# A 2:4-sparse matrix product on one core: the second token pair's load behind a memset, tile 4 transposed before tiles 2 and 3, one 512-column dummy matmul fewer

## The chip, the core and the metric

The kernel runs on one core of one Trainium2 chip. The metric is the device time of one execution in microseconds; lower is better. Where a number stands without a unit it is microseconds, counted from the start of the profiled span.

## What is computed

`x` is 16x512 tokens of 1024 bf16 values, `w` a 1024x1024 bf16 matrix, `b` a bias of 1024. In each column of `w`, of every four rows that follow each other the two of largest magnitude are kept; then the pruned matrix multiplies the tokens:

```python
wg = w.reshape(G, M, D)                       # G = 256 groups of M = 4 rows
mag = jnp.abs(wg)
order = jnp.argsort(mag, 1)
thr = jnp.take_along_axis(mag, order[:, M - N:M - N + 1, :], 1)   # N = 2
wp = (wg * (mag >= thr)).reshape(D, D)
return jnp.einsum("bsd,df->bsf", x, wp) + b
```

## The kernel before

The 8192 tokens are 64 tiles of 128 tokens. The product of a tile is two halves of 512 output columns, each the sum of eight matmuls over 128 of the 1024 inputs. The last 48 to 50 tiles (L359 to L375) run in one regular stream: tokens come in already transposed by DMA, TensorE multiplies, VectorE adds the bias while it empties the PSUM bank, and the result is stored.

The front handles the time in which the weights aren't pruned yet. The weights are cut into six pieces (L61): pieces 0 to 3 are rows 0 to 511 in steps of 256 columns, 4 and 5 rows 512 to 1023 in steps of 512. A piece is loaded (`load_w`, L69), its magnitudes taken (`abs_piece`, L109: token A), and pruned in place on VectorE (`prep_piece`, L124: token P; L150 makes the mask, L153 applies it). Piece 0 is pruned in two halves of the group index m (0 and 1, then 2 and 3), and the first half in two column blocks, so that the first matmuls can begin early.

The first eight token tiles are not transposed by DMA but by TensorE: `load_x` (L76) loads the first 512 inputs of one or two tiles in natural order (tiles 0 and 1, tiles 2 and 3, tile 4, tile 5, tiles 6 and 7), `transpose_half` (L177, token T) makes four 128x128 transposes with an identity matrix into a PSUM bank taken in turn by `next_bank` (L53), and `copy_half` (L184, token C) brings the bank back to SBUF on ScalarE. Tokens N and M are matmuls (`mm_part`, L191): N.0.t.m multiplies piece 0 with tile t for one group index m, M does all four. N.0.t.0 and N.0.t.1 read the first half of piece 0, N.0.t.2 and N.0.t.3 the second. Token V copies a finished half to a staging buffer on ScalarE (L235); token U unpacks the pruned piece into natural row order by DMAs on SP (L172); D and G are DMA transposes on SP (`xfill`, L259, and `xg1`, L324); I loads weights.

W and w are dummy matmuls (`warm`, L104) of ones into PSUM bank 7, with 512 and 128 columns. They read nothing that is loaded and nothing reads them.

What sets the order: `K` keeps the instructions that it wraps in program order, so every engine's queue follows the text: first the loads at L83 to L91, then the small set-up (a zeroed tile, a first copy on ScalarE with its table load, the identity, which GpSimd makes), then the tokens of the string FRONT (L285), one after the other. DMAs are issued by two queues: SP has the first half of the first weight piece (128 KB), tiles 0 and 1 (256 KB), tile 4, tile 5, the second weight piece, tiles 6 and 7, and more weights; ScalarE has the other half of the first weight piece and tiles 2 and 3 (256 KB).

Of the kernel before, what the change touches and what calls it, by code (L numbers as in the profile page):

```python
# [10 lines left out]
def kernel(  # L11
# [7 lines left out]
    nc = tc.nc  # L19
    P = 128  # L20
    bf16 = mybir.dt.bfloat16
# [4 lines left out]
    K = tc.keep_in_program_order  # L26

    B, S, D = x.shape
# [10 lines left out]
    T, F = 8, 6  # L39
    NE = 8  # L40

    const = ctx.enter_context(tc.tile_pool(name="const", bufs=1))
# [30 lines left out]

    xh = {}

    def load_x(ta, tb, eng=nc.sync):  # L76
        xt = const.tile([P, tb - ta, KH], bf16, name=f"xh_{ta}")
        src = xf[ta * P:tb * P, 0:KH].rearrange("(t p) c -> p t c", p=P)
        K(eng.dma_start(xt[:], src))
        for t in range(ta, tb):  # L80
            xh[t] = xt[:, t - ta, :]

    load_w(0, 0, 256, nc.sync, 0, 2)  # L83
    load_w(0, 0, 256, nc.scalar, 2, 4)
    load_x(0, 2)
    load_x(2, 4, nc.scalar)
    load_x(4, 5)
    load_x(5, 6)
    load_w(0, 256, 512)
# [4 lines left out]
    xg1 = const.tile([P, 4, T * P], bf16, name="xg1")  # L94

    ones = nc.const_aps.tensor(1.0, (P, FH), bf16)
    zeros = const.tile([P, 16], bf16, name="zeros")
    K(nc.vector.memset(zeros[:], 0.0))
    act_first = const.tile([P, 16], bf16, name="act_first")
    K(nc.scalar.copy(act_first[:], zeros[:]))  # L100
    ident = const.tile([P, P], bf16, name="ident")
    make_identity(nc, ident[:])

    def warm(n):  # L104
        K(nc.tensor.matmul(bank[7][:, :n], lhsT=ones[:, :P], rhs=ones[:, :n], start=True, stop=True))  # L105
# [160 lines left out]
    def issue_batch(t0, nb):  # L266
# [16 lines left out]


    FRONT = """  # L285
        I.1.0.512 D.0 A.0 P.0 W W W W W W W W W w w T.0 T.1 C.0 T.2 T.3 C.1 w T.4 C.2 N.0.0.0 N.0.0.1 T.5
        N.0.1.0 N.0.1.1 N.0.0.2 N.0.0.3 N.0.1.2 N.0.1.3 M.0.2 A.1 C.3 P.1 U.0.0.0.512 I.1.512.1024 G C.4 C.5
        M.0.3 N.0.4.0.1 T.6 T.7 C.6 N.0.4.2.3 C.7 A.2 M.0.5 M.0.6 P.2 M.0.7 N.1.0.0.1 N.1.1.0.1 A.3
        N.1.2.0.1 N.1.0.2.3 N.1.1.2.3 N.1.2.2.3 V.0.0 M.1.3 V.0.1 M.1.4 V.0.2 M.1.5 M.1.6 V.0.3 M.1.7 V.0.4
# [114 lines left out]
```

## Time and profile before

| | |
|---|---|
| median of 3 runs | 233.38 us (232.98 to 233.41) |
| profiled execution | 232.85 us, of which the span is 231.1 |
| TensorE busy | 226.7 us, 98% of the span |
| VectorE, ScalarE, GpSimd busy | 52%, 8%, under 1% |
| first dummy / first transpose / first matmul of real work | 0.77 / 4.78 / 6.38 us |
| loads of the first weight piece, issue to landing | 2.6 us (SP), 2.8 us (ScalarE) |
| loads of tiles 0 and 1 and of tiles 2 and 3, issue to landing | 3.4 us (SP), 3.8 us (ScalarE), both issued at 1.25 |
| bytes moved from 2.25 to 4.20 us | 339 GB/s |

How to read it: the profile is of one execution, which is faster than the median of the runs by 0.53. A group of matmuls in a timeline shows its start and the time until the end of the last; the starts inside a group are as far apart as the matmuls need at the current clock, and a single matmul's length (379 ns for 512 columns) holds the run through the array as well, so that neighbours overlap. The chain of what ended last counts from end to end instead. An idle engine that is not on that chain costs nothing.

### The profile page before, as it was taken

To read this page: it belongs to the slowest core of one execution; us is meant where nothing else is said; L and a number is where in the kernel's file an instruction comes from. 1 tells how busy PE (TensorE), PEld (TensorE's weight loads), DVE (VectorE), ACT (ScalarE), POOL (GpSimd) and SP (SyncE) were. 2 spreads that over 40 slices of the span, in tenths; PEclk is the share of its full clock that TensorE was granted. 3 is DMA by queue.
4 is the path that set the end of the run, shared out by engine and by line. 5 is a ranking of instruction groups with operands and counts; after the bars stand their busy time and mean duration, and the time that the engine had idled before them with its cause. 6 is when DMAs were issued, how large, how long until landed. Compare 5 with 4: busy or idle time off the path is not lost.

```text
span 231.1 us, 2772 instructions
## 1 busy us (share of the span) xinstructions
PE 226.7 (98%) x1137; PEld 111.1 (48%) x1156; DVE 120.2 (52%) x213; ACT 18.0 (8%) x33; POOL 0.7 (0%) x6
## 2 busy tenths in 40 slices
PE   8999999999999999999999999999999999999995
PEld 4887444444444444444444444444444444444443
DVE  4999787867987424424424424424423423433434
ACT  3868400000000000000000000000000000000000
POOL 1000000000000000000000000000000000000000
PEclk9999999999999999999999999999999999999999
DMA  6989989999447222991249522696128950122222
GB/s 214 299 180 262 210 195 197 289 247 318 185 182 272 91 84 80 272 249 59 80 115 278 152 95 91 129 245 194 70 91 197 241 197 34 60 91 91 91 94 91
DMA packets 77228, 38.19 MB, mean 165 GB/s; under 512 B 63136, under 2 KB 69024, under 8 KB 77216
## 3 DMA queue, kind: packets, MB, share of 16 engines
q1 hardware_dynamic: 67568, 20.88, 41.4%
q10 hardware_dynamic: 9648, 17.14, 20.1%
q8 instruction: 9, 0.15, 0.3%
q14 instruction: 3, 0.02, 0.0%
HBM read 3.41 MB, written 16.78 MB: 87 GB/s over the span
## 4 chain that ended last, share of the span: by engine, by line
PE 98%; DVE 0%; issue 0%
PE bank L369 73%; PE bank L203 16%; PE bank L263 6%; PE bank L105 2%; PE bank L182 1%; DVE o_last L354 0%
## 5 line engine op out<-in xcount | busy, mean ns | idle before, releaser
L369 PE MATMUL bank<-wp_nat,xTb 128*128 128x512 bf16 x737 | 161.7, 379 | 0.8
L248 DVE TENSOR_TENSOR o_pair<-bank,bias_sb 128x512 bf16<-128x512 f32 x104 | 67.3, 687 | 99.5 <-PE bank L369 94.1
L369 PEld LDWEIGHTS <-xTb 128*128 128x128 bf16 x752 | 73.6, 98 | 88.7
L239 DVE TENSOR_TENSOR stage<-bank,stage 128x512 f32<-128x512 f32 x22 | 14.2, 687 | 4.3 <-PE bank L203 4.2
L203 PE MATMUL bank<-w,xT 128*128 128x256 bf16 x128 | 14.5, 273 | 0.0
L243 DVE TENSOR_TENSOR o_pair<-stage,bias_sb 128x512 bf16<-128x512 f32 x22 | 14.0, 684 | 0.0
L203 PE MATMUL bank<-wp_nat,xg 128*128 128x512 bf16 x62 | 13.9, 379 | 0.1
L203 PEld LDWEIGHTS <-xT 128*128 128x128 bf16 x128 | 12.3, 98 | 1.6
L235 ACT COPY stage<-bank 128x512 f32<-128x512 f32 x22 | 11.5, 613 | 4.5 <-PE bank L203 4.5
L203 PE MATMUL bank<-wp_nat,xfill 128*128 128x512 bf16 x47 | 10.6, 379 | 0.1
L263 PE MATMUL bank<-wp_nat,xfill 128*128 128x512 bf16 x47 | 10.5, 379 | 0.1
L203 PEld LDWEIGHTS <-xg 128*128 128x128 bf16 x64 | 6.3, 98 | 7.6
L263 PEld LDWEIGHTS <-xfill 128*128 128x128 bf16 x48 | 4.7, 98 | 5.7
L203 PEld LDWEIGHTS <-xfill 128*128 128x128 bf16 x48 | 4.7, 98 | 5.5
L369 PE MATMUL bank<-wp_nat,xTs 128*128 128x512 bf16 x32 | 7.1, 379 | 0.0
L150 DVE TENSOR_TENSOR mask<-mag,thr 128x512 bf16<-128x512 bf16 (+3 forms) x10 | 5.6, 584 | 0.2
L153 DVE TENSOR_TENSOR w<-w,mask 128x512 bf16<-128x512 bf16 (+3 forms) x10 | 5.6, 582 | 0.1
L105 PE MATMUL bank<-const-bfloat16-1.0 128*128 128x512 bf16 (+1 forms) x12 | 4.4, 540 | 0.8 <-PEq L388 0.8
L369 PEld LDWEIGHTS <-xTs 128*128 128x128 bf16 x32 | 3.1, 98 | 3.8
L187 ACT COPY xT<-bank 128x512 bf16<-128x512 bf16 x8 | 4.1, 605 | 2.7 <-PE bank L182 2.7
L120 DVE TENSOR_SCALAR mag<-w 128x512 uint16<-128x512 uint16 (+2 forms) x6 | 2.7, 466 | 2.5 <-DMA w<-in_w_dram 2.5
L263 PE MATMUL bank<-wp_nat,xTb 128*128 128x64 bf16 (+3 forms) x40 | 3.7, 251 | 0.0
(20 smaller groups left out, 27.1 us busy)
## 6 DMA issues: line engine op xcount, KB each, us to landing
out_dram<-o_pair ACTq DMA_DIRECT2D x25, 512.0 KB, 2.8
out_dram<-o_pair ACTq DMA_DIRECT2D x13, 256.0 KB, 2.1
wp_nat<-w SPq DMA_DIRECT2D x16, 128.0 KB, 2.9
w<-in_w_dram SPq DMA_DIRECT2D x3, 512.0 KB, 5.5
xh<-in_x_dram SPq DMA_DIRECT2D x2, 256.0 KB, 4.1
xh<-in_x_dram ACTq DMA_DIRECT2D x1, 256.0 KB, 3.8
xh<-in_x_dram SPq DMA_DIRECT2D x2, 128.0 KB, 3.6
w<-in_w_dram SPq DMA_DIRECT2D x1, 256.0 KB, 4.0
```

What stands on the lines that cost most here:

```text
L105: K(nc.tensor.matmul(bank[7][:, :n], lhsT=ones[:, :P], rhs=ones[:, :n], start=True, stop=True))
L120: K(nc.vector.tensor_single_scalar(mag[:, ms].bitcast(u16), w_of(i)[:, ms].bitcast(u16), 0x7FFF, op=Alu.bitwise_and))
L150: K(nc.vector.tensor_tensor(mask[:, ms, c], mag[:, ms, c], tb, op=Alu.is_ge))
L153: K(nc.vector.tensor_tensor(w_of(i)[:, ms, c], w_of(i)[:, ms, c], mask[:, ms, c], op=Alu.mult))
L187: K(nc.scalar.copy(xt[:], src))
L203: K(nc.tensor.matmul(dst, lhsT=lhs, rhs=rhs, start=c0 == 0 and m == 0, stop=c1 == FH and m == 3))
L235: K(nc.scalar.copy(stage[(h, t)][:], bank[own[(h, t)]][:]))
L239: K(nc.vector.tensor_tensor(st, bank[own[(2 + h, t)]][:], st, op=Alu.add))
L243: K(nc.vector.tensor_tensor(get_o(t)[:, f], stage.pop((h, t))[:], bias_sb[:, f], op=Alu.add))
L248: K(nc.vector.tensor_tensor(get_o(t)[:, f], bank[bk][:], bias_sb[:, f], op=Alu.add))
L263: K(nc.tensor.matmul(bank[bk][:, :c1 - c0], lhsT=xN[t][:, kt, :], rhs=wp_nat[h][:, kt, c0:c1], start=kt == 0, stop=kt == KT - 1))
L369: K(nc.tensor.matmul(bank[bks[h]][:], lhsT=xN[t][:, kt, :], rhs=wp_nat[h][:, kt, :], start=kt == 0, stop=kt == KT - 1))
```

## The change

- `load_x` can put a memset of the whole tile (128 partitions x 1024 bf16) on GpSimd ahead of the load. The load of tiles 2 and 3 does so; since both write the same tile, the load, which stays in ScalarE's queue, waits for the memset.
- The identity, the zeroed tile and ScalarE's first copy move up ahead of that load in the text, and so in the queues of GpSimd, VectorE and ScalarE.
- In FRONT, nine 512-column dummies become eight; the three 128-column dummies stay. The copy of tile 0 follows its transposes at once (on another engine: the order on each engine is as before), the small third dummy comes after tile 1, and tile 4 is transposed before tiles 2 and 3, so tile 4 takes the third PSUM bank and tiles 2 and 3 the fourth and the fifth.

```diff
-    def load_x(ta, tb, eng=nc.sync):
+    def load_x(ta, tb, eng=nc.sync, behind=False):
         xt = const.tile([P, tb - ta, KH], bf16, name=f"xh_{ta}")
+        if behind:
+            K(nc.gpsimd.memset(xt[:], 0.0))
         src = xf[ta * P:tb * P, 0:KH].rearrange("(t p) c -> p t c", p=P)
         K(eng.dma_start(xt[:], src))
...
     load_x(0, 2)
-    load_x(2, 4, nc.scalar)
+    ident = const.tile([P, P], bf16, name="ident")
+    make_identity(nc, ident[:])
+    zeros = const.tile([P, 16], bf16, name="zeros")
+    K(nc.vector.memset(zeros[:], 0.0))
+    act_first = const.tile([P, 16], bf16, name="act_first")
+    K(nc.scalar.copy(act_first[:], zeros[:]))
+    load_x(2, 4, nc.scalar, behind=True)
     load_x(4, 5)
...
     ones = nc.const_aps.tensor(1.0, (P, FH), bf16)
-    zeros = const.tile([P, 16], bf16, name="zeros")
-    K(nc.vector.memset(zeros[:], 0.0))
-    act_first = const.tile([P, 16], bf16, name="act_first")
-    K(nc.scalar.copy(act_first[:], zeros[:]))
-    ident = const.tile([P, P], bf16, name="ident")
-    make_identity(nc, ident[:])
...
-        I.1.0.512 D.0 A.0 P.0 W W W W W W W W W w w T.0 T.1 C.0 T.2 T.3 C.1 w T.4 C.2 N.0.0.0 N.0.0.1 T.5
+        I.1.0.512 D.0 A.0 P.0 W W W W W W W W w w T.0 C.0 T.1 C.1 w T.4 T.2 T.3 C.2 N.0.0.0 N.0.0.1 T.5
```

## Prediction

> **What bounds the kernel now.** I read the page first (busy shares, chain that ended last), then the chain in order of time, then each engine's timeline over the first 14 us. The chain:
>
> ```profile
> PE 98%; DVE 0%; issue 0%
> ...
> 0.77 4.21 PE bank L105 x11
> 4.99 1.28 PE bank L182 x16
> ...
> 6.54 0.22 PE bank L203 x2
> 6.76 0.22 PE bank L182 x4
> 6.99 1.75 PE bank L203 x16
> ```
>
> Columns: start, length, what. TensorE is the chain from its first dummy (L105) to the end, through transposes (L182) and matmuls (L203 and later), with no piece of another engine until the last tile. So the change counts only through when TensorE can begin its real work, and by whether it stops somewhere. The start, TensorE's and VectorE's timelines:
>
> ```profile
> 0.77 4.21 PE L105 MATMUL bank<-const-bfloat16-1.0 128*128 128x512 bf16 x11 [0.77 <-PEq L388]
> 4.78 1.48 PE L182 MATMUL bank<-ident,xh 128*128 128x128 bf16 x16
> 6.10 0.22 PE L105 MATMUL bank<-const-bfloat16-1.0 128*128 128x128 bf16 x1
> 6.38 0.38 PE L203 MATMUL bank<-w,xT 128*128 128x256 bf16 x2
> 6.82 1.91 PE L203 MATMUL bank<-w,xT 128*128 128x256 bf16 x16
> ...
> 3.35 0.51 DVE L120 TENSOR_SCALAR mag<-w 128x512 uint16<-128x512 uint16 x2 [2.47 <-DMA w<-in_w_dram]
> 5.66 0.49 DVE L153 TENSOR_TENSOR w<-w,mask 128x256 bf16<-128x256 bf16 x2
> 6.52 0.43 DVE L153 TENSOR_TENSOR w<-w,mask 128x512 bf16<-128x512 bf16 x1
> ```
>
> Two chains meet. VectorE waits 2.47 us for the first weight loads and then prunes without a gap: the first half of piece 0 is ready at 5.66+0.49 = 6.15, the second at 6.52+0.43 = 6.95. TensorE needs the first half at 6.38 (N.0.0.0, 0.23 to spare) and the second at N.0.0.2, the third of the sixteen: 6.82 + 2x0.109 = 7.04 (1.75/16 = 0.109 each), so 0.09 to spare. This 0.09 is the tightest place I find: **TensorE and VectorE are both nearly the bound here**. The next pieces have more: piece 1 is pruned by 10.27 and used from 10.57 and 11.22 on.
>
> **The clock in these rows.** 9 dummies of 512 columns and 2 of 128 (38 units of 128) lie between 0.77 and 4.78: 0.106 a unit, 0.42 a large dummy. The matmuls of 256 columns after 7 us take 0.109, 0.055 a unit. So TensorE starts at half rate. The 16 transposes take 6.10-4.78 = 1.32 = 0.106n + 0.055(16-n), n = 8.6: the rate doubles at about 5.69.
>
> **The dummy.** One 512-column dummy goes (9 become 8; the three small ones stay): the transposes can start 0.42 earlier, at 4.36. Tiles 0 and 1, the small dummy and tile 4 are 13 units at 0.106, up to the step at 5.69: 5.72. Tiles 2 and 3 are 8 units at 0.055: 6.16. So N.0.0.0 could start at 6.16, 0.22 earlier (half of 0.42, since work moves from full rate to half rate). But the first half is ready at 6.15 and, 0.66 of TensorE work later, the second at 6.95: N.0.0.2 would be reached at 6.82 to 6.86 and starts between 6.95 and 7.0. **Gain 0.04 to 0.09; I take 0.06.** The rest of the 0.22 becomes a new wait for VectorE, since nothing in the change starts VectorE earlier: both weight loads are first in their queues.
>
> **The first pair.** Its weights are read from 4.72 and its load lands 3.4 us after 1.25, at 4.67: only 0.05 to spare, and it is now wanted at about 4.30. In the trace its packets share the 16 engines with the second pair's from about 3.2 on. Without those 256 KB before it ends (at the 339 GB/s of the stretch 2.25 to 4.20, up to 0.77 us; some two thirds had gone, 0.5) it lands near 4.15. Bounds: 4.67, unchanged (TensorE then stands out the 0.42 of the dummy, and the 0.06 is not gained), and 3.9, all 0.77 earlier. I take 4.15: no cost.
>
> **The second pair's load.** ScalarE and GpSimd:
>
> ```profile
> 1.25 0.52 ACTq L79 DMA_DIRECT2D xh<-in_x_dram  x1
> 1.79 1.28 ACT L100 ACT_TABLE_LOAD   x1 [1.79 <-issue]
> 3.09 0.20 ACT L100 COPY act_first<-zeros 128x16 bf16<-128x16 bf16 x1
> ...
> 0.34 0.10 POOL L388 MEMSET const-uint8-127<- 128x1 uint8 x1
> 0.73 0.21 POOL masks.py:197 MEMSET ident<- 128x128 bf16 x1 [0.29 <-POOLq L388]
> 1.01 0.29 POOL masks.py:199 TENSOR_SCALAR_AFFINE_SELECT ident<-ident 128x128 bf16<-128x128 bf16 x1
> ```
>
> It moves behind the table load and the first copy on ScalarE's queue: 1.25+1.28 = 2.53, +0.20 = 2.73, so it is issued at 2.6 to 2.75. The memset (128x1024) is not in the trace. From 0.10 for 1 element a partition and 0.21 for 128, 1024 give 0.10+1023x0.00087 = 0.98: done at 1.30+0.98 = 2.28, before ScalarE asks, so this wait would cost nothing of its own. Ends: 0.21 (length without effect), and eight times the select's 0.29, 2.3, done at 3.64. Nearest is the memset row; I take 0.98. From issue to landing the trace has 2.1 us (a store of 256 KB from the same queue, later, alone) to 4.7 (the slowest load of x). I take 2.1 plus 0.77 for as many bytes of other loads that share the engines, 2.87: it **lands at about 5.6**, wanted at 5.72. Earliest 2.6+2.1 = 4.7; latest 3.64+4.7 = 8.3. Behind it on ScalarE nothing stands until the copies of tiles 0 and 1 (at 5.0 and 5.5), whose place comes after its issue.
>
> **The rest at nothing.** The identity moves no work: GpSimd has it at 1.30, wanted at 4.3. Tile 4 before 2 and 3 gives it the third PSUM bank; that bank is emptied by the fifth of the eight copies of L235 (from 11.64, 0.48 apart: by 14.2) and taken again at 14.9. SP's first DMA transpose (5.38) carries in its record a wait on the semaphore that the second pair raises. Landing at 5.6 to 6 holds SP for 0.2 to 0.6, and with it the unpacking, the next weights and the xg transpose behind it. xfill lands at 5.38+9.9 = 15.3 for a first use at 20.9, xg at 15.88+7.2 = 23.1 for 26.0: 2.9 cover it. The memset's zeros are overwritten by the load.
>
> **Sum.** The profiled execution took 232.85 (span 231.1 and 1.75 around it): 232.85-0.06 = 232.8. The shown runs (232.98 to 233.41, median 233.38) lie 0.53 above; off their median it is **233.3**, no change. 0.2% (0.47 us) is about what a measurement of this kernel can tell from none.
>
> **Rivals.**
> 1. *The pair comes late (slower).* Place: tile 2's weight load behind tile 4. TensorE loses nothing against before up to a landing at 7.04-0.66-0.44 = 5.94, and from there us for us. At 6.4 it is 0.47 (233.9); at the far end, 8.3, it is 2.4 (235.8). For it: the load shares with x 4, x 5 and 256 KB of weights; its old time was 3.8, which from 2.7 gives 6.5 (0.6 lost, 234.0). Against: a third of that was its place behind the weights on its queue. 0.2 for over 0.47.
> 2. *The clock steps up later (slower).* If TensorE stands before 5.69, for either pair, and the step needs unbroken work, half rate lasts longer. In this trace it lasted 4.9 us from the first dummy; as much again would cost half of it, 2.4: 235.8. Decides if a stop of some tenths before 5.69 is enough; the trace has no such stop. 0.08. The Trainium skill ("TensorE: Matmul & The Clock Gate", Part 1) says that the gate opens after a busy window of 3.4 us that runs free of the kernel; by it the price would be half of 3.4, 1.7 us (235.1), and the warm-up is a matter of time, not of dummies. The trace's 4.9 us agrees with one whole window after a part of one; it can't show what a gap does.
> 3. *The runs shown suffer from the first pair (faster).* With 0.05 to spare in an execution 0.53 faster than the median, the first pair may land up to 0.5 late in the others, with TensorE standing. Taking the second pair away would end that: 233.38-0.53-0.06 = 232.8, 0.25% faster. Against: late weight loads explain the 0.53 as well, and these the change leaves alone. 0.22.
> 4. *It doesn't delay.* Were the load still issued at 1.25, only the dummy would count and TensorE would wait for the first pair in its place: 233.4, inside the forecast.
>
> **Numbers.** Forecast with rival 4: 0.5, between 232.9 and 233.8. Faster 0.22, slower 0.28 (rivals 1 and 2). The range 232.7 to 234.3 takes in rival 3 and rival 1 up to a landing at 6.9; it leaves out rival 2 and the far end of the memset.
>
> **What the profile would show.** Right: transposes from 4.36; the second pair's issue near 2.7, landing near 5.6; a small wait of TensorE for VectorE's L153 ahead of N.0.0.2; N.0.0.2 near 6.97. Wrong: TensorE waiting for xh before tile 0 or tile 2; a memset much over 1 us; the rate doubling later than 5.7; VectorE's first instruction off 3.35, which would move everything by as much.

## The result and the profile after

The changed kernel takes 240.17 us (median of 6 runs, 239.96 to 241.42), the kernel before beside it 233.28 (232.98 to 233.45): ratio 1.0307, 95% interval 1.0285 to 1.0330. It is slower by 6.9 us; the forecast was 233.3 within 232.7 to 234.3. The span of the profiled execution went from 231.1 to 238.3, by 7.2. Two lines of the page carry it, the chain by engine and the issue of the second pair's load (out<-in, queue, KB, us to landing):

```profile
PE 94%; DMA 4%; DVE 0%; SPq 0%; issue 0%; ACTq 0%
...
xh<-in_x_dram ACTq DMA_DIRECT2D x1, 256.0 KB, 7.1
```

TensorE was 98% of the chain before and is 94% now, with a DMA for 4%. The chain in order of time (start, length, what) says which:

```profile
1.25 3.40 DMA xh<-in_x_dram
4.65 0.02 issue
4.67 0.02 ACTq L81
4.69 0.04 issue
4.73 7.11 DMA xh<-in_x_dram
11.84 0.05 issue
11.89 1.04 PE bank L184 x8
...
13.78 2.22 PE bank L205 x16
```

Read it from below. TensorE's transposes of tiles 2 and 3 start at 11.89, when their load has landed (4.73+7.11 = 11.84). That load was issued at 4.73, and what released ScalarE's queue at 4.67 was not GpSimd: it was the landing, at 1.25+3.40 = 4.65, of the load of tiles 0 and 1. GpSimd's row shows the memset done at 1.24+0.95 = 2.19:

```profile
1.24 0.95 POOL L79 MEMSET xh<- 128x1024 bf16 x1
```

Why ScalarE waits for another load: the program's loads share eight counting semaphores (100, 103, 105 to 110 in the records of the changed kernel's trace), which a DMA raises when it lands. They are handed out in turn, in the order in which the scheduler of the program places the DMAs. Before the change this load is the third and raises one that no DMA has used yet (104). In the changed kernel, with the memset behind the identity on GpSimd, its number is the eleventh, after nine of SP's; it gets the semaphore of tiles 0 and 1 (105), and the program lets it raise that one only after its first user has landed: ScalarE's record at 4.67 is a wait on 105, and the load behind it raises 105.

The stretches between 2.25 and 11.8 (us, then busy time of each engine, granted clock, DMA share, GB/s), before the change:

```profile
3.25:5.00 1.75, 1.75 (x9) 0.87 (x8) 1.66 (x9) 0.04 (x1) 0.00 (x0) 1.00 1.05 346
5.00:8.00 3.00, 3.00 (x38) 2.87 (x37) 2.93 (x13) 2.55 (x6) 0.00 (x0) 1.00 1.02 312
```

and after:

```profile
3.25:5.00 1.75, 1.59 (x10) 0.75 (x9) 1.54 (x8) 0.00 (x0) 0.00 (x0) 1.00 0.85 215
5.00:8.00 3.00, 0.81 (x11) 0.48 (x9) 2.02 (x11) 1.07 (x2) 0.00 (x0) 0.97 0.83 223
8.00:11.80 3.80, 0.00 (x0) 0.00 (x0) 3.41 (x11) 0.00 (x0) 0.00 (x0) 0.50 1.09 317
```

Three things stand here: the engines move less (346 to 215, then 312 to 223 GB/s), TensorE does nothing from 8.0 to 11.8, and its granted clock is 0.50 by then.

**Theory.** The wait for the borrowed semaphore moves the issue from 1.25 to 4.73; there it stands behind loads of SP's that were issued after 2.7, so landing takes 7.1 in place of 3.8; and the stop of 6 us closes TensorE's clock gate (the throttle that grants it full or half rate). **Rivals:** the memset or ScalarE's queue position is slow in itself; the first DMA transpose holds the load's packets back; the missing dummy and the new order of tiles cost something.

### The profile page after: what moved, and what is told of

It is laid out like the page before. It is cut to its first block, busy times and chain, and to the rows that moved or that the text cites. A ratio compares the mean times of both kernels' runs of the same rounds, so it can differ in the third digit from the quotient of the medians.

```text
span 238.3 us, 2791 instructions
## 1 busy us (share of the span) xinstructions
PE 228.7 (96%) x1155; PEld 111.5 (47%) x1155; DVE 120.4 (51%) x213; ACT 18.1 (8%) x33; POOL 1.6 (1%) x7
## 4 chain that ended last, share of the span: by engine, by line
PE 94%; DMA 4%; DVE 0%; SPq 0%; issue 0%; ACTq 0%
PE bank L371 71%; PE bank L205 16%; PE bank L265 5%; DMA xh<-in_x_dram 4%; PE bank L184 1%; DVE o_last L356 0%; SPq L71 0%; ACTq L81 0%
## 5 line engine op out<-in xcount | busy, mean ns | idle before, releaser
L205 PE MATMUL bank<-w,xT 128*128 128x256 bf16 x128 | 15.3, 280 | 0.0
L184 PE MATMUL bank<-ident,xh 128*128 128x128 bf16 x32 | 3.3, 256 | 6.2 <-DMA xh<-in_x_dram 6.2
L184 PEld LDWEIGHTS <-xh 128*128 128x128 bf16 x32 | 2.6, 127 | 6.9 <-DMA xh<-in_x_dram 6.8
L135 DVE TENSOR_TENSOR hi<-mag 128x512 bf16<-128x512 bf16 (+2 forms) x7 | 3.1, 462 | 3.4 <-ACT mag L119 3.2
```

The lines of the kernel that those rows point to most:

```text
L135: K(nc.vector.tensor_tensor(hi[:, a], magv[:, a, 0, :], magv[:, a, 1, :], op=Alu.max))
L184: K(nc.tensor.transpose(dst[:, m, :], xv[:, m, :], ident[:]))
L205: K(nc.tensor.matmul(dst, lhsT=lhs, rhs=rhs, start=c0 == 0 and m == 0, stop=c1 == FH and m == 3))
```

## The experiments

**1. No memset** (`nomemset`).

```diff
-    load_x(2, 4, nc.scalar, behind=True)
+    load_x(2, 4, nc.scalar)
```

> The changed kernel without the memset; all else as changed, the load's place behind ScalarE's table load and first copy included. Theory (the memset makes the scheduler give this load the completion semaphore of the load of tiles 0 and 1, so ScalarE issues it only when that one has landed, at 4.73, behind 1 MB of weights and a DMA transpose): issue at 2.6 to 2.8, landing 5.6 to 6.5, TensorE stops under 1 us for it, 233.0 to 234.2. Rival (the later place in ScalarE's queue is enough, since whatever ScalarE issues after 2.5 us is crowded out): landing after 8, over 235.5.

233.16 beside 232.99, ratio 1.0012 (0.9994 to 1.0029): all of the loss is gone (one of its 11 runs took 235.06, the others 232.78 to 233.44). The issue isn't where either theory put it. ScalarE's timeline:

```profile
1.26 1.28 ACT L93 ACT_TABLE_LOAD   x1 [1.26 <-PEq L390]
1.32 0.44 ACTq L81 DMA_DIRECT2D xh<-in_x_dram  x1
2.55 0.20 ACT L93 COPY act_first<-zeros 128x16 bf16<-128x16 bf16 x1
```

The DMA stands behind the table load and the copy in the program and is issued at 1.32, while the table load runs: they do not hold it. Tiles 2 and 3 land at 5.06 (5.05 before the change). So the place in ScalarE's queue is worth nothing, and the rival that it crowds the load out falls. The run says nothing of an issue at 2.7, which needed another kernel (experiment 5).

**2. FRONT alone** (`front_only`): the kernel before with only the changed line of FRONT.

> The kernel before with the changed FRONT alone (one large dummy fewer, tile 4 before tiles 2 and 3); loads, set-up and memset as before. Theory: the first pair still lands near 4.67, so that the dummy's 0.42 turns into a wait for it, and nothing else moves: 233.1 to 233.5. Rival (fewer dummies or the gap delay the step of the clock, and that is part of the 7 us): over 234.5.

233.08 beside 232.99, ratio 1.0001 (0.9991 to 1.0011): neither dummy nor order costs or gains more than 0.1%.

**3. The DMA transpose later** (`late_transpose`); R loads 2 KB that nothing reads.

```diff
-        I.1.0.512 D.0 A.0 P.0 ...
+        I.1.0.512 R A.0 P.0 ...
-        ... U.0.0.0.512 I.1.512.1024 G ...
+        ... U.0.0.0.512 D.0 I.1.512.1024 G ...
```

> The changed kernel with the first DMA transpose (xfill) moved behind the unpacking DMAs on SP's queue, and in its old place a load of one 2 KB row that nothing reads, so that the second pair's load keeps the same semaphore and is issued at 4.7 as in the changed kernel. If the transpose is what holds its packets back: first packets near 5.8, landing 7 to 8, time 235 to 237. If the 1 MB of weights ahead on SP's queue does it: landing stays 11 to 12, time 239 to 241.

Its one run took 241.02: issue at 4.52, 7.0 to landing (11.56). The transpose alone is not what holds the load back.

**4. The gap filled** (`filled_gap`): 24 dummies W between T.4 and T.2.

> The changed kernel with 24 more 512-column dummies between tile 4 and tile 2, where TensorE stands for the load of tiles 2 and 3 (about 5.2 us of them at full rate, so they end before it lands near 11.8). If the stop also closed the clock gate: tiles 2 and 3 and the first matmuls run at full rate, 1.2 to 1.4 less than the changed kernel, 238.7 to 239.1. If the stop costs only its own length: 240.0 to 240.4.

238.88, 1.29 less than the changed kernel, with the load landing as late as there (4.41 issued, 7.2 later). The stretch 12.0 to 14.4 in the changed kernel and here:

```profile
12.00:14.40 2.40, 2.40 (x18) 2.06 (x18) 2.30 (x9) 1.86 (x4) 0.00 (x0) 0.50 0.95 197
```

```profile
12.00:14.40 2.40, 2.40 (x30) 2.22 (x28) 2.19 (x7) 2.06 (x4) 0.00 (x0) 1.00 1.00 184
```

TensorE starts 18 matmuls at a clock of 0.50 there and 30 at 1.00 here. So the stop closed the gate, and that is 1.3 of the 7.2; in the profiled runs the load also landed 0.2 earlier here, which may be part of the 1.3.

The Trainium skill ("TensorE: Matmul & The Clock Gate", Part 1) has the gate close after an idle window of some 3.4 us and open after a busy one. The trace agrees that a stop closes the gate and that work opens it, but not on these lengths: TensorE's last matmul before the stop ends at 6.14, the 0.97 of the row from 5 to 8 puts the fall of the granted clock at about 7.8, 1.7 later, and the half rate lasts from 11.89 to about 14.6, 2.7 of work. In `bare_queue` (experiment 7) a stop of 2.4 was already enough.

**5. The issue time alone.** Three kernels change only when the load is issued; two of them keep its own semaphore, by making the memset ahead of the identity.

```diff
-            K(nc.gpsimd.memset(xt[:], 0.0))
+            for _ in range(1):        # issue_1_7; 2 in issue_2_7
+                K(nc.gpsimd.memset(xt[:], 0.0))
...
-    ident = const.tile([P, P], bf16, name="ident")
-    make_identity(nc, ident[:])
     zeros = const.tile([P, 16], bf16, name="zeros")
...
     load_x(2, 4, nc.scalar, behind=True)
+    ident = const.tile([P, P], bf16, name="ident")
+    make_identity(nc, ident[:])
```

`issue_3_6` has the changed kernel's order with four memsets by VectorE (`nc.vector.memset`); it borrows the semaphore of ScalarE's weight load.

> The changed kernel with the memset ahead of the identity on GpSimd, so that the load of tiles 2 and 3 waits for the memset alone and raises a semaphore of its own; issue at about 1.7. Theory (what counts is when the load is issued; the later it is, the more of SP's loads go ahead of it): landing 5.2 to 5.9, 233.0 to 233.6. Rival (a load that waits for a GpSimd memset is itself slow): landing after 8, over 235.5.

> As the last, with the memset made twice: the load waits for GpSimd alone and is issued at about 2.65, the moment that the prediction took. By the prediction's step (2.87 from issue to landing): landing 5.5 to 5.9, 233.0 to 233.5. By the backlog theory (what SP issued before it goes first, in one order for both queues): landing 6.5 to 8, 233.8 to 235.5.

> The changed kernel with four memsets on VectorE in place of one on GpSimd (VectorE is idle until 3.3): the load then takes the semaphore of ScalarE's weight load and is issued when that has landed, at about 3.6. By the prediction's step: landing 6.5 to 7, 233.6 to 234.2. By the backlog theory: landing 8 to 10, 235.3 to 237.5.

| kernel | issued | to landing | landed | span | median, ratio (interval) |
|---|---|---|---|---|---|
| before | 1.25 | 3.8 | 5.05 | 231.1 | 232.95 |
| issue_1_7 | 1.72 | 5.0 | 6.76 | 233.5 | 235.33, 1.0083 (1.0054 to 1.0111) |
| issue_2_7 | 2.75 | 4.0 | 6.74 | 232.0 | 234.39, 1.0074 (1.0043 to 1.0105) |
| issue_3_6 | 3.57 | 6.8 | 10.39 | 237.8 | 239.42, 1.0272 (1.0247 to 1.0297) |
| changed | 4.73 | 7.1 | 11.84 | 238.3 | 240.17, 1.0307 (1.0285 to 1.0330) |

The landing does not follow the issue in step: issue_1_7 and issue_2_7 are issued 1.0 apart and land together, and from 2.75 to 3.57 it jumps, 0.8 later issued, 3.65 later landed. Part of this is the spread between the 16 DMA engines, since a load has landed when its last engine is done. The first engine is done at 4.72 before the change and at 4.79 in issue_1_7, the last at 5.05 and 6.76; in issue_2_7 it is 5.88 and 6.74, in issue_3_6 6.75 and 10.39. issue_2_7 agrees with the backlog (6.74 in 6.5 to 8), not with the prediction's 5.6. issue_1_7 is a miss for both sides: a delay of 0.5 already costs 1.7 of landing, more than my theory's 5.2 to 5.9 and less than the rival's 8. issue_3_6 landed later than either expected.

The spans follow the prediction's rule, us for us from a landing at 5.94, plus half of what runs at half rate after a stop: for the changed kernel 11.84-5.94 = 5.90 and 1.3 make 7.2, the measured difference; for issue_2_7 0.80 for 0.9; for issue_1_7 0.82, and half rate from its landing to about 10.0, 1.6, make 2.4 for 2.4; for issue_3_6 4.45, and half rate from 10.43 to about 15.1, 2.3, make 6.75 for 6.7.

The runs of issue_2_7 fall in two groups, 233.68 to 233.78 and 235.00 to 236.01, and the profiles of issue_2_7 and issue_1_7, whose loads land at the same time, show one of each. The second line is the first sixteen matmuls in a row:

```profile
7.26 0.38 PE L206 MATMUL bank<-w,xT 128*128 128x256 bf16 x2
...
7.70 1.91 PE L206 MATMUL bank<-w,xT 128*128 128x256 bf16 x16
```

```profile
7.65 0.63 PE L206 MATMUL bank<-w,xT 128*128 128x256 bf16 x2
...
8.50 2.66 PE L206 MATMUL bank<-w,xT 128*128 128x256 bf16 x16
```

1.91 for the sixteen in issue_2_7, 2.66 in issue_1_7, where the rate doubles only about halfway through them. In issue_1_7's profile that is the prediction's second rival, a first step that comes late: its granted clock reads 1.000 on average, as the upper run of 235.00 does. The other three upper runs of issue_2_7 read 0.993, half rate for about 3.3 of 234 us, which the record shows only after a first step: an estimate from that number is that there the short stop closed the gate again. Either way the price is 1.3 to 2.3 a run.

**6. TensorE kept busy** (`issue_2_7_busy`): issue_2_7 with W in place of the small dummy ahead of T.4, and two W ahead of T.2.

> issue_2_7 (memset twice, load issued at 2.75) whose runs fell into two groups, near 233.7 and from 235.0 to 236.0; here with one large dummy in place of the small one ahead of tile 4 and two large ones ahead of tile 2, so that TensorE doesn't stand while it waits. If the second group is the clock stepping up a window later after a stop: no run over 234.4, median 233.5 to 234.1. If the load itself lands in two groups: still several runs over 235.

234.10 (233.79 to 234.71), ratio 1.0040 (1.0026 to 1.0054). No run is over 235, and the granted clock is 1.000 in all six: the upper group is gone, as the clock theory has it, but two runs are over the 234.4 that it allowed. The landing itself varies: in this profile it is 4.9 after the issue at 2.75, 7.7, against 6.74 in experiment 5, and the span is 232.9.

**7. SP's later loads out of the way** (`bare_queue`). The load of 0, 512 to 1024 and the tokens I.1.0.512 and D.0 stand behind U.0.0.0.512; three R, of 512 bytes each, keep the count of semaphores.

```diff
-    load_w(0, 512, 1024)
...
-        I.1.0.512 D.0 A.0 P.0 ...
+        R.0 R.1 R.2 A.0 P.0 ...
-        ... U.0.0.0.512 I.1.512.1024 G ...
+        ... U.0.0.0.512 I.0.512.1024 I.1.0.512 D.0 I.1.512.1024 G ...
```

> The changed kernel with two weight loads (1 MB) and the first DMA transpose moved behind the unpacking on SP's queue; in their places loads of 512 bytes that nothing reads, so that the load of tiles 2 and 3 keeps its semaphore and its issue at 4.5 to 4.8. Its time is not to be compared, since those weights come late; what counts is that load. If the bytes that SP issued just before go first: it lands 2.5 to 3.8 after its issue. If not: 6 to 7.5 after, as in the changed kernel.

```profile
xh<-in_x_dram ACTq DMA_DIRECT2D x1, 256.0 KB, 3.7
...
5.49 0.42 PE L183 MATMUL bank<-ident,xh 128*128 128x128 bf16 x4 [0.27 <-DMA xh<-in_x_dram]
8.32 1.04 PE L183 MATMUL bank<-ident,xh 128*128 128x128 bf16 x8 [2.41 <-DMA xh<-in_x_dram]
```

Issued at 4.56, in one run, and 3.7 to landing in place of 7.1. In the changed kernel SP issues 1 MB at 4.10 and 4.71, half of it ahead of this load and half beside it, and then the transpose. Without both, the other 3.4 are gone, though the load has ScalarE's queue to itself: its first packet runs 1.8 after the issue (6.40), in the changed kernel 3.7 after (8.43). Experiment 3 moved the transpose alone and gained nothing, so the 1 MB is needed for the delay; the 1 MB moved alone was not run. The two lines of TensorE show the gate again: four transposes at full rate, a stop of 2.41, and eight at half rate.

**8. One queue** (`one_queue`): no memset, and `load_x(2, 4)` on SP.

> The changed kernel without the memset and with the load of tiles 2 and 3 on SP's queue, right behind tiles 0 and 1. In the changed kernel the 16 DMA engines moved 215 GB/s from 3.25 to 5.0 where the kernel before moved 346. If that is because SP alone issues too few bytes then (128 KB each half microsecond): the rate returns to 310 to 350, tiles 2 and 3 land near 5.2 and tile 4 near 5.7, 233.0 to 233.8. If one queue can't fill the engines: at most 260 GB/s, tiles 2 and 3 after 5.8, tile 4 after 6.4, over 234.0.

234.32, ratio 1.0050 (1.0036 to 1.0063). From 3.25 to 5.0 the engines move 276 GB/s, between the two expectations; tiles 2 and 3 land 4.3 after their issue at about 1.74, at 6.0. More bytes issued early by SP bring back some of the rate of the kernel before the change, 346, but not all. This run does not settle why, and the number of queues is not it: with loads on both queues issue_1_7 moves 228 in this stretch and issue_2_7 199, while nomemset, whose second pair is issued at 1.32, moves 351.

## Why the prediction was wrong

- **The step that failed is "The second pair's load".** Its issue was put at 2.6 to 2.75 and was 4.73; its way to landing at 2.87 (at most 4.7) and was 7.1. It landed at 11.84, beyond the far end of 8.3.
- The issue failed by a wait that the step didn't look for. The prediction named the mechanism one paragraph on, for SP's transpose, which waits on the semaphore that this load raises; it didn't ask whether the load, moved behind another engine, would itself be given a used one. The two rows that it did use were off without effect: the memset took 0.95 (0.98 was taken), and ScalarE's table load holds no DMA issue (experiment 1).
- The way to landing failed because a quiet row was scaled: a store that had the engines to itself, plus one share for company. With 1 MB of SP's loads ahead and beside it that is 7.1, and without them and the transpose 3.7 (experiment 7).
- **Rival 1 was the right case and its price was right**: nothing lost up to 5.94, then us for us. It was given 0.2 for over 0.47, and its far end of 8.3 was too near.
- **The clock came on top of it**, but not as rival 2 has it. Rival 2 is a first step that comes late, and that is what issue_1_7's profile shows (experiment 5). In the changed kernel the first step was early (tiles 0 and 1 are transposed at full rate from 4.70, eight in 0.64); the stop closed the gate again, for 1.3 (experiment 4), below the 2.4 and 1.7 of rival 2.
- The step at 5.69, on which the working of the dummy rests, is that of one execution and not of the kernel. The same eight transposes take 0.64 from 4.70 in the changed kernel and from 4.75 in nomemset, at full rate, and 1.04 from 4.67 in front_only and from 4.38 in filled_gap, at half rate.
- Rival 4's price was right where its condition was met: with the load issued at 1.25 and 1.32, front_only took 233.08 and nomemset 233.16 (233.4 forecast). Rival 3 was not tested.
- The first pair: forecast to land at 4.15 without the second's 256 KB beside it; 4.65 in the changed kernel, the "unchanged" end, but 4.33 in filled_gap, whose loads are the same up to there, and 4.2 in issue_1_7 and issue_2_7. So the 4.15 was near what some executions show. What the step did not expect is that the engines then moved 215 GB/s in place of 346.
- The dummy and the order of the tiles: no gain, as the bound for an unchanged first pair had it (experiment 2). The 0.06 was not seen.
- VectorE's first instruction on the weights came at 3.46 (3.35), and its next weights kept it waiting for 0.95 at 8.0; behind TensorE's stop of 6 us neither mattered.

Open: why the engines move only 223 GB/s from 5 to 8 us in the changed kernel, with SP's loads waiting; and why the landing in issue_1_7 is 1.7 late for a delay of 0.5. In both the 16 engines finish one load far apart (in the changed kernel first to last 1.6 to 2.8 for SP's loads that land from 6 to 12, against 0.3 for most of the early ones before the change), but what sets a single engine back isn't seen.

## What to carry to other kernels

An edit that makes a DMA wait for another engine can change more than that wait: where completion semaphores are taken in turn, look up in the compiled program, or in the trace's records, which one the DMA gets and whose landing it must then wait for. A load's time to landing is not its own property; count the bytes issued ahead of it and beside it on every queue, since a load moved 3.5 us later here met 1 MB more. And a stop of TensorE is priced twice when it is long enough to close the clock gate: the wait, and half of the half-rate time after it (here 5.9 and 1.3).

## What the runs showed of the hardware that was not expected

- A DMA issue on ScalarE's queue is not held by an activation table load that started before it: issued at 1.32 while the table load ran from 1.26 to 2.54 (nomemset), and at 1.72 while it ran from 1.25 to 2.53 (issue_1_7).
- From 3.25 to 5.0 the engines moved 346 GB/s with the second pair on ScalarE's queue from 1.25 on, 215 with it issued at 4.73, and 276 with it on SP's queue. The Trainium skill ("DMA: Bandwidth & Descriptors", Issuing engines are not separate DMA queues) says that a second issuing engine saves only issue time. These runs do not speak against it, since two queues also moved as little as 199 (issue_2_7, with the pair issued at 2.75); what makes the 346 is open.
- The granted clock reads 1.00 in the first 5 us, where matmuls run at half rate (0.427 between dummies of 512 columns); it shows 0.50 only after a stop (6 us in the changed kernel, 2.4 in bare_queue). In issue_1_7 it reads 1.00 from 5 to 11, though the rate doubles only near 10. The distance between matmuls is the safer sign.
